# Attention in three-product precision: low parts on another engine, some squares on ScalarE, scores three blocks ahead, and the next batch prepared over two chunks

## The chip, the cores and the metric

The kernel runs on one core of a Trainium2 chip. A core has TensorE (PE, with its weight loads, PEld), VectorE (DVE), ScalarE (ACT), GpSimd (POOL) and SyncE (SP), each with its own queue that it works off in order, and DMA engines. Engines wait for each other by semaphores. The metric is the device time of one execution in microseconds; the kernel before takes 1697.85 us, the median of three runs (1695.41 to 1698.38).

## The reference

There is an attention without softmax, then two mixture-of-experts layers on its output:

```python
scores = scale * np.matmul(z, z.transpose(0, 2, 1))    # z: 4 x 3072 x 64, scale = 1/3072
attn = np.maximum(scores, 0.0) ** 2
x = u * np.matmul(attn, v)                              # u, v: 4 x 3072 x 256
logits = x @ moe_w_gate                                 # then a routing of 12288 tokens by capacity,
h = np.maximum(x[mask] @ w1[e], 0.0); y = h @ w2[e]     # 8 experts, and a second such layer
```

All tensors are fp32. The change touches the attention alone.

## The kernel before

**Precision.** A fp32 factor is split into a high part in TensorE's rounded fp32 format (fp32r) and a low part, the difference. A product is then three matmuls: high by high, low by high, high by low. So each of z, v, the squared scores and x has a copy on ScalarE (the high part: zHL's upper half, pH, aH, xH) and a subtraction (the low part: zHL's lower half, pL, aL, xL).

**Tiling.** The attention runs over 24 chunks: four batches of six chunks of 512 queries each. A chunk goes over 24 blocks of 128 keys (KT). For a block, `scores` makes two matmuls into a PSUM tile sc (zHL holds high part over low part, zLH the same two swapped), then r = relu(scale * sc) on ScalarE (L371), the full square a on VectorE (L377), the rounded square aH on ScalarE (L379) and aL = a - aH on VectorE (L381). `av` makes six matmuls into two accumulators (L396 aH by the high part of v, L397 aL by the high part, L398 aH by the low part, for two halves of d). After the 24th block VectorE multiplies each accumulator by u into xT (L400).

**What sets the order.** The program is recorded step by step, with no scheduler. Step s emits `scores(s + 2)`, then `av(s)`, then whatever a table of hooks holds for step s; each engine keeps that order. At the last block of a chunk the scores stand between the two halves (L401). Buffers: two of sc, r and a, four of aH and aL.

**Hooks of a chunk.** `turn_u` (a 32x32-block transpose of u on VectorE), `load_u`, `swap_z` (two DMAs from GpSimd's queue that make zLH of the next chunk), and of the chunk that has just ended `part_x` (xH on ScalarE, xL on GpSimd, L331), `logits` (four matmuls), `turn_l`, `put_l`, `put_x` (for the first ten chunks with two transposes rowb on VectorE). In the last chunk of a batch come the six z tiles and six v tiles of the next batch: `load_z`, `part_z` (VectorE transpose zT), `turn_z` (copy on ScalarE, low part on GpSimd, L281), `load_v`, `part_v` (copy pH on ScalarE L234, low part pL on GpSimd L235). The first batch's tiles are prepared in the first chunk in the same way, v in four pieces a tile. zHL and pH/pL have eight buffers, six for a batch and two to spare.

**The last batch** (chunks 18 to 23) also carries the first steps of the routing. There, blocks with an odd number have their full square on ScalarE (L375), so that VectorE has only aL. In the last chunk VectorE also splits four weight tiles of 128x1024 (at L235, with the copy on ScalarE).

Of the kernel before, what the change touches and what calls it, by code (L numbers as in the profile page):

```python
# [8 lines left out]
F32 = mybir.dt.float32  # L9
FR = mybir.dt.float32r  # L10
BF = mybir.dt.bfloat16
I32 = mybir.dt.int32
AF = mybir.ActivationFunctionType
OP = mybir.AluOpType
# [64 lines left out]
class Moe:  # L79
# [174 lines left out]
    def _attention(self, W, u, v, z, gates, stages, hooks):  # L254
        nc, S, B = self.nc, self.S, self.B
        KT, QC = S // 128, S // 512
        NC = B * QC
        zr, zT, zHL, vr, V, zLH, uraw, uT, xT, row, xp, lg = ({} for _ in range(12))

        def at(s, f, *a):  # L260
            hooks.setdefault(s, []).append((f, a))
# [13 lines left out]
        def turn_z(b, i):  # L275

            t = zHL[b, i] = W.tile([128, 512], FR, name="zHL", bufs=QC + 2)
            first = b == i == 0
            eng = nc.vector if first else nc.gpsimd
            nc.scalar.activation(t, zT[b, i], AF.Copy)  # L280
            eng.tensor_tensor(t[64:128], zT[b, i][64:128], t[64:128].bitcast(F32), OP.subtract)  # L281
            if first:
                l = zLH[0] = W.tile([128, 512], FR, name="zLH", bufs=2)
                nc.scalar.activation(l, zT[b, i], AF.Copy)
                eng.tensor_tensor(l[0:64], zT[b, i][0:64], l[0:64].bitcast(F32), OP.subtract)  # L285

        def swap_z(c):
            b, q = divmod(c, QC)
# [6 lines left out]
        VS = [128, 4, 256]  # L295
# [2 lines left out]
            vr[b, i] = self.load(v[b].rearrange("(i t p) d -> i p t d", p=128, t=4)[i], VS)  # L298

        def part_v(b, i):  # L300
            V[b, i] = self.split(vr[b, i], VS, nc.gpsimd, self.w, b == 0)

        def load_u(c):
            b, q = divmod(c, QC)
# [21 lines left out]
        def part_x(c, h):  # L326
            H = self.w.tile([128, 512], FR, name="xH", bufs=1)
            nc.scalar.activation(H, xT[c][:, h], AF.Copy)  # L328
            L = self.w.tile([128, 512], FR, name="xL", tag="xL", bufs=1)
            eng = nc.gpsimd if c < NC - 1 else nc.vector  # L330
            eng.tensor_tensor(L, xT[c][:, h], H.bitcast(F32), OP.subtract)  # L331
            xp[c, h] = H, L

        def logits(c, h):
# [25 lines left out]
        SCALE = 1.0 / S  # L360
        HS, LS = {}, {}

        def scores(s):
            c, k = divmod(s, KT)
            b = c // QC
            p = self.sc()
            lw = zHL[b, k // 4][:, k % 4 * 128:(k % 4 + 1) * 128]
            nc.tensor.matmul(p, lw, zHL[b, c % QC], start=True, stop=False)  # L368
            nc.tensor.matmul(p, lw, zLH[c], start=False, stop=True)  # L369
            r = W.tile([128, 512], F32, name="r", bufs=2)  # L370
            nc.scalar.activation(r, p, AF.Relu, scale=SCALE)  # L371
            a = W.tile([128, 512], F32, name="a", bufs=2)
            if b == B - 1 and k % 2:

                nc.scalar.activation(a, r, AF.Square)  # L375
            else:
                nc.vector.tensor_tensor(a, r, r, OP.mult)  # L377
            HS[s] = W.tile([128, 512], FR, name="aH", bufs=4)
            nc.scalar.activation(HS[s], r, AF.Square)  # L379
            LS[s] = W.tile([128, 512], FR, name="aL", bufs=4)  # L380
            nc.vector.tensor_tensor(LS[s], a, HS[s].bitcast(F32), OP.subtract)  # L381

        accs = None
# [1 line left out]
        def av(s):  # L385
            nonlocal accs
            c, k = divmod(s, KT)
            b = c // QC
            if k == 0:
                accs = [self.acc(), self.acc()]  # L390
            vh, vl = V[b, k // 4]
            if k == KT - 1:
                xT[c] = self.w.tile([128, 2, 512], F32, name="xT", bufs=1)
            for h in range(2):
                sl = (slice(None), k % 4, slice(h * 128, (h + 1) * 128))
                nc.tensor.matmul(accs[h], vh[sl], HS[s], start=k == 0, stop=False)  # L396
                nc.tensor.matmul(accs[h], vh[sl], LS[s], start=False, stop=False)  # L397
                nc.tensor.matmul(accs[h], vl[sl], HS[s], start=False, stop=k == KT - 1)  # L398
                if k == KT - 1:
                    nc.vector.tensor_tensor(xT[c][:, h], accs[h], uT[c][:, h], OP.mult)  # L400
                    if h == 0 and s + 2 < NS:  # L401
                        scores(s + 2)

        def put_l(c):
            for q in range(4):
# [3 lines left out]
        NS = NC * KT  # L409
        load_z(0, 0)  # L410
        load_v(0, 0)
        self.warm(12, self.mi())
        part_z(0, 0)
        turn_z(0, 0)
        load_z(0, 1)
        load_v(0, 1)
        load_u(0)
        part_v(0, 0)
        part_z(0, 1)
        tables = self.consts(*gates)  # L420
# [3 lines left out]
        for i in range(1, QC):  # L424
            d = 2 * (i > 2)
            at(4 * i - 4 - d, turn_z, 0, i)
            if i > 1:
                at(4 * i - 6 - d, part_z, 0, i)
                at(4 * i - 8 - d, load_z, 0, i)
                at(4 * i - 8, load_v, 0, i)  # L430
            at(4 * i - 3, part_v, 0, i)
        for c in range(NC):
            s0 = c * KT
            b, q = divmod(c, QC)
            if c + 1 < NC:
                at(s0 + 17, load_u, c + 1)
                at(s0 + 13, swap_z, c + 1)
            at(s0 + 12, turn_u, c, 0)
            at(s0 + 16, turn_u, c, 1)
            if c + 1 < NC:  # L440
                e = s0 + KT
                for t, f, a in ((0, part_x, (0,)), (2, logits, (0,)), (3, part_x, (1,)), (5, logits, (1,)),
                                (6, turn_l, ()), (8, put_l, ()), (9, put_x, ())):
                    at(e + t, f, c, *a)
            if q == QC - 1 and b + 1 < B:
                for i in range(QC):
                    at(s0 + 1 + 3 * i, load_z, b + 1, i)
                    at(s0 + 6 + 3 * i, part_z, b + 1, i)
                    at(s0 + 8 + 3 * i, turn_z, b + 1, i)
                    at(s0 + 4 * i - 6, load_v, b + 1, i)  # L450
                    at(s0 + 4 * i + 2, part_v, b + 1, i)
        for s in range(2):
            scores(s)
        for s in range(NS):
            if s + 2 < NS and s % KT != KT - 1:
                scores(s + 2)
            av(s)
            for f, a in hooks.pop(s, []):
                f(*a)
            for s0, p, c in stages:  # L460
                if p.done:
                    continue
                if s0 is None:

                    j = self.JP + 4 * (p.n // 5)
                    if s < (j // 4 + 1) * KT + 10:
                        break
                if s0 is None or s >= s0:
                    p.step(c)
                break  # L470
            if getattr(self, "pend", None):
                self.put_tail()
        for _, p, _ in stages:
            p.finish()
        c = NC - 1
        return [lambda: part_x(c, 0), lambda: (logits(c, 0), part_x(c, 1)), lambda: logits(c, 1),
                lambda: turn_l(c), lambda: put_x(c)]

# [1124 lines left out]
```

## Time and profile before

| | |
|---|---|
| median of three runs | 1697.85 us |
| profiled execution | 1710.32 us, its span 1708.5 us |
| TensorE busy | 1609.7 us, 94% of the span |
| VectorE busy | 1320.4 us, 77% |
| ScalarE busy | 1037.5 us, 61% |
| GpSimd busy | 508.8 us, 30% |
| mean granted TensorE clock | 0.982 of full speed |

How to read it: a share of busy time is a mean over stages. Matmuls are pipelined and a record of one (0.39 us) overlaps the next, so the pace of TensorE is read from the starts of neighbours (0.23 us), not from the lengths. The same holds for VectorE and ScalarE, whose records overlap by less than 0.1 us. The stretches below are cut where the second xT of a chunk ends; chunks are counted from 0, so that 5, 11 and 17 are those in which the next batch is prepared.

### The profile page before, as it was taken

How to read it: one execution, taken by the hardware profiler on the slowest of the kernel's cores; microseconds unless marked ns; L12 is line 12 of the kernel's file. 1: busy time of each engine (PE TensorE's matmuls, PEld its weight loads, DVE VectorE, ACT ScalarE, POOL GpSimd, SP SyncE). 2: the span in 40 equal slices, each digit the busy share in tenths (PEclk: the TensorE clock that was granted, in tenths of full speed). 3: DMA queues.
4: the chain of work that ended last, by engine and by line, in shares of the span. 5: the costliest groups of instructions: out<-in, count | busy, mean ns of one | idle time of the engine just before them, and what ended most of it. 6: DMA issues, size and time to landing. Idle time of an engine off the chain costs nothing.

```text
span 1708.5 us, 24999 instructions
## 1 busy us (share of the span) xinstructions
PE 1609.7 (94%) x8568; PEld 1323.5 (77%) x8570; DVE 1320.4 (77%) x2387; ACT 1037.5 (61%) x1777; POOL 508.8 (30%) x629
## 2 busy tenths in 40 slices
PE   8999998999999899999889999999999959999997
PEld 5788875788887588888667777767888849987997
DVE  8888889888888888888887777667777765776662
ACT  7666666666666566666677767766434315654552
POOL 6411014111112411011430278752333213324341
PEclk9999999999999999999999999999999969998999
DMA  5111255223224322212410111114334303553530
GB/s 124 29 29 31 41 144 132 56 76 78 70 56 107 85 56 57 56 45 48 105 40 13 33 33 37 26 41 134 107 107 126 99 15 101 185 163 101 162 122 31
DMA packets 282680, 132.43 MB, mean 78 GB/s; under 512 B 216717, under 2 KB 268173, under 8 KB 282544
## 3 DMA queue, kind: packets, MB, share of 16 engines
q1 hardware_dynamic: 269264, 106.90, 24.7%
q0 software_dynamic: 13280, 23.85, 4.8%
q8 instruction: 69, 1.13, 0.3%
q14 instruction: 67, 0.55, 0.1%
HBM read 84.61 MB, written 40.55 MB: 73 GB/s over the span
## 4 chain that ended last, share of the span: by engine, by line
PE 70%; DVE 19%; issue 4%; ACT 3%; POOL 1%; DMA 0%; another core or an unknown queue 0%; SPq 0%; DVEq 0%; POOLq 0%; ACTq 0%
PE acc L397 13%; PE acc L398 12%; PE acc L396 12%; PE sc L1010 9%; PE sc L368 6%; PE sc L369 6%; DVE aL L381 6%; PE acc L1160 5%; DVE a L377 5%; PE mi L1111 1%; ACT r L371 1%; DVE pL L225 1%; PE mi L338 1%; PE rt L863 1%; DVE hL L1020 1%
## 5 line engine op out<-in xcount | busy, mean ns | idle before, releaser
L371 ACT ACTIVATE r<-sc 128x512 f32<-128x512 f32 x576 | 343.6, 596 | 335.1 <-PE sc L369 300.5
L381 DVE TENSOR_TENSOR aL<-a,aH 128x512 fp32r<-128x512 f32 x576 | 447.4, 778 | 125.4 <-ACT aH L379 41.6
L397 PE MATMUL acc<-aL,pH 128*128 128x512 f32 x1152 | 460.5, 400 | 43.4 <-DVE aL L381 40.6
L377 DVE TENSOR_TENSOR a<-r 128x512 f32<-128x512 f32 x504 | 401.2, 796 | 70.2 <-ACT r L371 65.1
L396 PE MATMUL acc<-aH,pH 128*128 128x512 f32 x1152 | 451.6, 392 | 0.1
L398 PE MATMUL acc<-aH,pL 128*128 128x512 f32 x1152 | 451.4, 392 | 0.0
L379 ACT ACTIVATE aH<-r 128x512 fp32r<-128x512 f32 x576 | 363.3, 631 | 16.0
L397 PEld LDWEIGHTS acc<-aL,pH 128*128 128x128 f32 x1152 | 217.4, 189 | 120.5 <-DVE aL L381 75.6
L396 PEld LDWEIGHTS acc<-aH,pH 128*128 128x128 f32 x1152 | 217.5, 189 | 48.3 <-DVE xT L400 1.2
L398 PEld LDWEIGHTS acc<-aH,pL 128*128 128x128 f32 x1152 | 217.6, 189 | 42.9
L331 POOL TENSOR_TENSOR xL<-xT,xH 128x512 fp32r<-128x512 f32 x46 | 67.0, 1455 | 567.8 <-ACT xH L328 532.2
L368 PE MATMUL sc<-zHL 128*128 128x512 f32 x576 | 230.0, 399 | 5.4 <-ACT r L371 4.0
L369 PE MATMUL sc<-zLH,zHL 128*128 128x512 f32 x576 | 225.8, 392 | 0.2 <-DVE zLH L285 0.2
L1018 ACT ACTIVATE hH<-sc 128x432 fp32r<-128x432 f32 (+2 forms) x192 | 89.5, 469 | 216.6 <-PE sc L1010 201.4
L1020 DVE SCALAR_TENSOR_TENSOR hL<-sc,hH 128x432 fp32r<-128x432 f32 (+2 forms) x192 | 98.9, 523 | 67.6 <-ACT hH L1018 66.7
L368 PEld LDWEIGHTS sc<-zHL 128*128 128x128 f32 x576 | 109.1, 189 | 35.0 <-ACT r L371 4.8
L1010 PE MATMUL sc<-xTH,pH 128*128 128x384 f32 (+2 forms) x368 | 126.6, 344 | 7.0 <-DVE hL L1020 6.7
L369 PEld LDWEIGHTS sc<-zLH,zHL 128*128 128x128 f32 x576 | 109.0, 189 | 22.2 <-DVE zLH L285 0.5
L1010 PE MATMUL sc<-xTL,pH 128*128 128x384 f32 (+2 forms) x368 | 120.0, 326 | 0.0
L1010 PE MATMUL sc<-xTH,pL 128*128 128x384 f32 (+2 forms) x368 | 119.8, 326 | 0.0
L633 POOL DMA_INDIRECT tt<-TP,hidx x92 | 100.9, 1097 | 53.5 <-DVE ntail L653 25.8
L225 DVE TENSOR_TENSOR pL<-raw,pH 128x1024 fp32r<-128x1024 f32 x80 | 97.6, 1220 | 10.3 <-ACT pH L220 9.6
(335 smaller groups left out, 2153.0 us busy)
## 6 DMA issues: line engine op xcount, KB each, us to landing
raw<-in_moe_w_dram SPq DMA_DIRECT2D x84, 512.0 KB
raw<-in_v_dram SPq DMA_DIRECT2D x24, 512.0 KB
uraw<-in_u_dram SPq DMA_DIRECT2D x192, 64.0 KB
out_dram<-zt SPq DMA_DIRECT2D x24, 512.0 KB
xb<-xT SPq DMA_DIRECT2D x14, 512.0 KB
zr<-in_z_dram SPq DMA_DIRECT2D x96, 64.0 KB
zLH<-zHL POOLq DMA_DIRECT2D x46, 128.0 KB
ya<-zt SPq DMA_DIRECT2D x10, 544.0 KB
```

Of the source, the lines that this page charges most:

```text
L225: self.nc.vector.tensor_tensor(l, raw, h.bitcast(F32), OP.subtract)
L368: nc.tensor.matmul(p, lw, zHL[b, c % QC], start=True, stop=False)
L369: nc.tensor.matmul(p, lw, zLH[c], start=False, stop=True)
L371: nc.scalar.activation(r, p, AF.Relu, scale=SCALE)
L377: nc.vector.tensor_tensor(a, r, r, OP.mult)
L379: nc.scalar.activation(HS[s], r, AF.Square)
L381: nc.vector.tensor_tensor(LS[s], a, HS[s].bitcast(F32), OP.subtract)
L396: nc.tensor.matmul(accs[h], vh[sl], HS[s], start=k == 0, stop=False)
L397: nc.tensor.matmul(accs[h], vh[sl], LS[s], start=False, stop=False)
L398: nc.tensor.matmul(accs[h], vl[sl], HS[s], start=False, stop=k == KT - 1)
L1010: nc.tensor.matmul(p, a, b[:, d, :w], start=i == 0, stop=i == 5)
L1020: self.later.append(lambda: nc.vector.scalar_tensor_tensor(hL, p, 0.0, hH.bitcast(F32), op0=OP.max, op1=OP.subtract))
```

## The change

- The low parts of z, v and x are subtracted on VectorE instead of GpSimd, in all chunks.
- ScalarE makes the full square of every second block in the first chunk, in the last chunk of each batch and in the last batch (there as before), and of every third block elsewhere (k % 3 == 1). In these blocks aH now stands in front of a.
- `scores` runs three blocks ahead (LA) instead of two. aH and aL keep their four buffers.
- The hooks of the next batch are spread: the first z and v tile come 19 and 16 blocks before the last chunk of the batch begins, the second 6 and 3 before it, the other four within it, four blocks apart. `turn_z` comes one block after `part_z` instead of two. The distance from a load to its use stays five blocks for z and eight for v.

```diff
-            eng = nc.vector if first else nc.gpsimd
             nc.scalar.activation(t, zT[b, i], AF.Copy)
-            eng.tensor_tensor(t[64:128], zT[b, i][64:128], t[64:128].bitcast(F32), OP.subtract)
+            nc.vector.tensor_tensor(t[64:128], zT[b, i][64:128], t[64:128].bitcast(F32), OP.subtract)
...
         def part_v(b, i):
-            V[b, i] = self.split(vr[b, i], VS, nc.gpsimd, self.w, b == 0)
+            V[b, i] = self.split(vr[b, i], VS, nc.vector, self.w, b == 0)
...
-            eng = nc.gpsimd if c < NC - 1 else nc.vector
-            eng.tensor_tensor(L, xT[c][:, h], H.bitcast(F32), OP.subtract)
+            nc.vector.tensor_tensor(L, xT[c][:, h], H.bitcast(F32), OP.subtract)
...
+        LA = 3
...
-            if b == B - 1 and k % 2:
-
+            HS[s] = W.tile([128, 512], FR, name="aH", bufs=LA + 1)
+
+            if k % (2 if c == 0 or c % QC == QC - 1 or b == B - 1 else 3) == 1:
+                nc.scalar.activation(HS[s], r, AF.Square)
                 nc.scalar.activation(a, r, AF.Square)
             else:
                 nc.vector.tensor_tensor(a, r, r, OP.mult)
-            HS[s] = W.tile([128, 512], FR, name="aH", bufs=4)
-            nc.scalar.activation(HS[s], r, AF.Square)
-            LS[s] = W.tile([128, 512], FR, name="aL", bufs=4)
+                nc.scalar.activation(HS[s], r, AF.Square)
+            LS[s] = W.tile([128, 512], FR, name="aL", bufs=LA + 1)
             nc.vector.tensor_tensor(LS[s], a, HS[s].bitcast(F32), OP.subtract)
...
-                    if h == 0 and s + 2 < NS:
-                        scores(s + 2)
+                    if h == 0 and s + LA < NS:
+                        scores(s + LA)
...
                 for i in range(QC):
-                    at(s0 + 1 + 3 * i, load_z, b + 1, i)
-                    at(s0 + 6 + 3 * i, part_z, b + 1, i)
-                    at(s0 + 8 + 3 * i, turn_z, b + 1, i)
-                    at(s0 + 4 * i - 6, load_v, b + 1, i)
-                    at(s0 + 4 * i + 2, part_v, b + 1, i)
-        for s in range(2):
+                    t = s0 + (4 * i - 7 if i > 1 else 13 * i - KT + 5)
+                    at(t - 5, load_z, b + 1, i)
+                    at(t, part_z, b + 1, i)
+                    at(t + 1, turn_z, b + 1, i)
+                    at(t - 5, load_v, b + 1, i)
+                    at(t + 3, part_v, b + 1, i)
+        for s in range(LA):
             scores(s)
```

The order of VectorE at the end of chunk 4 and the first blocks of chunk 5 (a and aL are a block's square and its low part, zT, zHL, pL and xL belong to the preparation and to the chunk that ended). Before, from the first xT on:

```order
L400 TENSOR_TENSOR xT<-acc,uT 128x512
L377 TENSOR_TENSOR a<-r 128x512
L381 TENSOR_TENSOR aL<-a,aH 128x512
L400 TENSOR_TENSOR xT<-acc,uT 128x512
L377 TENSOR_TENSOR a<-r 128x512
L381 TENSOR_TENSOR aL<-a,aH 128x512
```

And now, from the same place:

```order
L401 TENSOR_TENSOR xT<-acc,uT 128x512
L379 TENSOR_TENSOR a<-r 128x512
L382 TENSOR_TENSOR aL<-a,aH 128x512
L401 TENSOR_TENSOR xT<-acc,uT 128x512
L382 TENSOR_TENSOR aL<-a,aH 128x512
L329 TENSOR_TENSOR xL<-xT,xH 128x512
L379 TENSOR_TENSOR a<-r 128x512
L382 TENSOR_TENSOR aL<-a,aH 128x512
L273 STREAM_TRANSPOSE zT<-zr 128x512
L382 TENSOR_TENSOR aL<-a,aH 128x512
L280 TENSOR_TENSOR zHL<-zT,zHL 64x512
```

Between the pairs of a and aL there now stand the low parts, and every second square is gone; before, that stretch goes on with six more pairs and nothing between them.

The order of ScalarE at the start of the program, from the first block's r to the copy of the second z tile. Before:

```order
L371 ACTIVATE r<-sc 128x512
L379 ACTIVATE aH<-r 128x512
L371 ACTIVATE r<-sc 128x512
L379 ACTIVATE aH<-r 128x512
L371 ACTIVATE r<-sc 128x512
L379 ACTIVATE aH<-r 128x512
L280 ACTIVATE zHL<-zT 128x512
```

And now:

```order
L371 ACTIVATE r<-sc 128x512
L380 ACTIVATE aH<-r 128x512
L371 ACTIVATE r<-sc 128x512
L376 ACTIVATE aH<-r 128x512
L377 ACTIVATE a<-r 128x512
L371 ACTIVATE r<-sc 128x512
L380 ACTIVATE aH<-r 128x512
L371 ACTIVATE r<-sc 128x512
L376 ACTIVATE aH<-r 128x512
L377 ACTIVATE a<-r 128x512
L279 ACTIVATE zHL<-zT 128x512
```

The copy stands behind four blocks and two full squares instead of behind three blocks.

## Rows read from the trace of the kernel before

**Rows 1.** Windows view: stretch; us, busy PE PEld DVE ACT POOL; PEclk, DMA, GB/s.

```profile
0.00:64.42 64.42, 56.93 (x219) 38.82 (x220) 55.14 (x69) 45.63 (x90) 40.78 (x52) 1.00 0.46 95
...
199.21:244.13 44.92, 44.80 (x197) 36.40 (x196) 38.24 (x56) 30.50 (x51) 4.71 (x5) 1.00 0.42 98
244.13:305.63 61.50, 49.52 (x200) 35.64 (x199) 58.20 (x62) 40.06 (x64) 30.93 (x18) 1.00 0.51 120
...
529.86:592.09 62.23, 50.77 (x196) 37.17 (x195) 57.37 (x61) 39.48 (x63) 30.88 (x18) 0.95 0.41 98
...
816.80:877.79 60.99, 50.38 (x199) 36.76 (x198) 56.35 (x59) 40.06 (x65) 30.94 (x18) 0.97 0.30 66
...
1132.07:1177.83 45.76, 44.83 (x198) 34.86 (x197) 35.13 (x60) 36.66 (x62) 26.71 (x39) 1.00 0.26 81
```

**Rows 2.** Waits view, 244.13 to 305.63 (engine line waited for: us, times, longest).

```profile
PE acc L397 <- DVE aL L381: 11.9, 11, 2.5
```

**Rows 3.** Lines view, 244.13 to 305.63 (columns: busy us, mean ns; idle us).

```profile
L377 DVE TENSOR_TENSOR a<-r 128x512 f32<-128x512 f32 x25 | 28.6, 1146 | 0.2 <-ACT r L371 0.2
L381 DVE TENSOR_TENSOR aL<-a,aH 128x512 fp32r<-128x512 f32 x24 | 24.7, 1028 | 3.1
...
L235 POOL TENSOR_TENSOR pL<-raw,pH 128x1024 fp32r<-128x1024 f32 x6 | 14.8, 2462 | 10.2 <-ACT pH L234 7.5 <-DVE a L377 2.6
```

**Rows 4.** Lines view, 484.93 to 529.86, an ordinary chunk.

```profile
L377 DVE TENSOR_TENSOR a<-r 128x512 f32<-128x512 f32 x25 | 17.8, 711 | 3.6 <-ACT r L371 3.4
L381 DVE TENSOR_TENSOR aL<-a,aH 128x512 fp32r<-128x512 f32 x24 | 17.6, 734 | 3.1
```

**Rows 5.** Timeline, 244 to 250 (start us, us, engine, line, operation).

```profile
248.46 2.41 POOL L235 TENSOR_TENSOR pL<-raw,pH 128x1024 fp32r<-128x1024 f32 x1 [2.57 <-DVE a L377]
248.56 2.85 DVE L381 TENSOR_TENSOR aL<-a,aH 128x512 fp32r<-128x512 f32 x1
```

**Rows 6.** Timeline of VectorE, undisturbed, near 255.

```profile
254.67 0.69 DVE L381 TENSOR_TENSOR aL<-a,aH 128x512 fp32r<-128x512 f32 x1
255.28 0.69 DVE L377 TENSOR_TENSOR a<-r 128x512 f32<-128x512 f32 x1
256.10 0.69 DVE L381 TENSOR_TENSOR aL<-a,aH 128x512 fp32r<-128x512 f32 x1
```

**Rows 7.** Timeline of ScalarE, 276 to 284.

```profile
277.94 1.04 ACT L234 ACTIVATE pH<-raw 128x1024 fp32r<-128x1024 f32 x1
278.89 0.58 ACT L371 ACTIVATE r<-sc 128x512 f32<-128x512 f32 x1
279.50 0.63 ACT L379 ACTIVATE aH<-r 128x512 fp32r<-128x512 f32 x1
280.04 0.58 ACT L371 ACTIVATE r<-sc 128x512 f32<-128x512 f32 x1
```

**Rows 8.** Timeline of VectorE, 1155 to 1180, a weight tile split.

```profile
1158.78 1.23 DVE L235 TENSOR_TENSOR pL<-raw,pH 128x1024 fp32r<-128x1024 f32 x1 [0.26 <-ACT pH L234]
1159.92 0.68 DVE L377 TENSOR_TENSOR a<-r 128x512 f32<-128x512 f32 x1
```

**Rows 9.** Timeline of TensorE behind the start of chunk 4.

```profile
201.05 0.39 PE L396 MATMUL acc<-aH,pH 128*128 128x512 f32 x1
...
201.56 0.50 PE L397 MATMUL acc<-aL,pH 128*128 128x512 f32 x1
...
201.90 0.40 PE L398 MATMUL acc<-aH,pL 128*128 128x512 f32 x1
```

**Rows 10.** Timeline of TensorE at the start of the program.

```profile
10.76 0.50 PE L397 MATMUL acc<-aL,pH 128*128 128x512 f32 x1 [0.70 <-DVE aL L381]
```

**Rows 11.** Waits view, 877.79 to 1177.83, the last six chunks.

```profile
PEld acc L397 <- DVE aL L381: 6.2, 10, 1.2
```

**Rows 12.** Timeline of VectorE at the start of the program.

```profile
6.17 0.69 DVE L281 TENSOR_TENSOR zHL<-zT,zHL 64x512 fp32r<-64x512 f32 x1 [0.70 <-ACT zHL L280]
6.89 0.69 DVE L285 TENSOR_TENSOR zLH<-zT,zLH 64x512 fp32r<-64x512 f32 x1
```

More of the change, by code (lines that the diff above doesn't have):

```diff
@@ L284, in turn_z @@
                 nc.scalar.activation(l, zT[b, i], AF.Copy)
-                eng.tensor_tensor(l[0:64], zT[b, i][0:64], l[0:64].bitcast(F32), OP.subtract)
+                nc.vector.tensor_tensor(l[0:64], zT[b, i][0:64], l[0:64].bitcast(F32), OP.subtract)
         def swap_z(c):
@@ L446, in _attention @@
                 for i in range(QC):
-                    at(s0 + 1 + 3 * i, load_z, b + 1, i)
-                    at(s0 + 6 + 3 * i, part_z, b + 1, i)
-                    at(s0 + 8 + 3 * i, turn_z, b + 1, i)
-                    at(s0 + 4 * i - 6, load_v, b + 1, i)
-                    at(s0 + 4 * i + 2, part_v, b + 1, i)
-        for s in range(2):
+                    t = s0 + (4 * i - 7 if i > 1 else 13 * i - KT + 5)
[5 more added lines that the diff above has]
+        for s in range(LA):
             scores(s)
         for s in range(NS):
-            if s + 2 < NS and s % KT != KT - 1:
-                scores(s + 2)
+            if s + LA < NS and s % KT != KT - 1:
+                scores(s + LA)
             av(s)
```

## The prediction

> **What bounds the kernel now.** I read the windows view first, cut where each chunk's second xT ends. A chunk that does nothing but attention (chunk 4 of the 24) takes 44.92 us, and TensorE is busy for 44.80 of it; the three chunks that also prepare the next batch take 61.50, 62.23 and 60.99; the first one ends at 64.42 [rows 1]. So in ordinary chunks TensorE is the bound, and nothing that the other engines save there counts, except where a wait stands. Together the three batch ends lose 184.72 - 3 x 44.92 = 50.0 us. The waits view of the first of them puts it on one place: L397, which needs aL, waits 11.9 us for VectorE's L381 [rows 2]. The lines view says why aL is late. There the square on VectorE (L377) takes 1146 ns on average and the low part (L381) 1028; in an ordinary chunk they take 711 and 734 [rows 3, 4]. That is 25 x 0.435 + 24 x 0.294 = 17.9 us of stretch, near the 16.6 us that this chunk loses. The timeline shows what stretches them: while GpSimd runs one low part of v for 2.41 us, the aL that starts 0.1 us after it takes 2.85 us, where an undisturbed one takes 0.69 [rows 5, 6]. GpSimd is busy for 30.93 us in this chunk, 14.8 of them with the six low parts of v, and for 4.71 in an ordinary one [rows 1, 3].
>
> **The change, part by part.**
>
> *Low parts of z, v, x to VectorE, preparation begun a chunk earlier, every second full square to ScalarE.* These act on the same 50.0 us, so I go by what each engine would have to do in such a chunk, in start-to-start times. VectorE: a block with both operations takes 0.82 + 0.61 = 1.43 [rows 6], a block whose square is ScalarE's 0.61. With twelve of each: 24.5. Two xT, two uT, one lgb, two rowb and two xL at 0.61 to 0.63: 5.6. Of the next batch four tiles are left in this chunk (two went to the one before): four zT 2.5, four low parts of z 2.4, four of v at 1.14 [rows 8] 4.6. Sum 39.6 of 44.92. ScalarE: r 0.61 and aH 0.54 per block, 27.6; twelve more squares at 0.54, 6.5; two xH 1.1, four copies of z 2.2, four of v at 0.95, 3.8 [rows 7]. Sum 41.2 of 44.92. Both fit as a whole. The tight part is the first 17 blocks (30.9 us of TensorE at 0.227 a matmul and eight a block, 31.8 with the logits and the chunk's start), since all of the preparation stands in them: VectorE 17 x 1.02 + 15 x 0.62 + 4.6 = 31.2, ScalarE 17 x 1.42 + 7.0 = 31.1. That is 98%, with the lead of three blocks on top of it. The nearest row that exists is the last chunk: there VectorE already has four tiles of this size to split, and ScalarE already makes every second square; it takes 45.76, 0.8 us over an ordinary one, with a lead of only two blocks [rows 1]. The new chunk has four z tiles and two xL more, so I leave 1.5 us of loss in each of the three: gain 50.0 - 4.5 = 45.5. Bounds: 50.0 if nothing is left, and 29 if the first 17 blocks' work queues so badly that 7 us stay in each.
>
> The moved instructions include DMA issues. SP gets to the z and v loads of the next batch up to a chunk earlier, in the same order of tiles and with the same distance to their use (five blocks for z, eight for v); buffers of z and v for the first two tiles are the two spare ones, so these loads wait for nobody. The chunk before takes two tiles: VectorE 16 x 1.43 + 8 x 0.61 + 5.6 + 4.8 = 38.1, ScalarE 27.6 + 8 x 0.54 + 1.1 + 3.0 = 36.0. It stays under TensorE's 44.92, and I cost it at nothing; if that cover failed, it would be a few us in each of three chunks.
>
> Against it, the Trainium skill ("VectorE: DVE Perf Modes", "Two Vector instructions with no wait between them") says that a VectorE instruction whose operand starts in another group of 32 partitions than the last one's starts only when all earlier ones have finished. The low part of z is on partitions 64 to 127. The trace agrees at the start of the kernel: behind it the next begins 0.72 us later, not 0.61 [rows 12]. By that, four such tiles would add about 8 x 0.11 = 0.9 us, and VectorE's 31.2 in the tight part would be 32.1. I leave the sum alone and give the first rival a little more.
>
> *Two xL of the ordinary chunks.* 23 chunks hand 46 of these to VectorE, at 0.61. Ordinary VectorE work is then 16 x 1.43 + 8 x 0.61 + 5.6 = 33.3 of 44.92, hidden beside TensorE. What goes is the stall at the chunk's start: GpSimd's xL stretches an aL there, and TensorE's next two starts are 0.51 and 0.34 after each other instead of 0.23 [rows 9], 0.39 us in each of the 14 ordinary chunks (1 to 4, 6 to 10, 12 to 16). Gain 5.5; bounds 0 and 5.5.
>
> *Scores three blocks ahead.* TensorE does the same matmuls. From the scores of a block to its use there are now 5.4 us and not 3.6, and the chain in between (r, square, low part) is about 3. So a stall below some 2 us disappears wherever VectorE and ScalarE catch up. In the last six chunks the weight load of L397 waits 6.2 us for aL [rows 11]; about 0.7 of such a wait reaches TensorE (0.39 of 0.55 in rows 9). Gain 4, bounds 0 and 6. Between the buffers nothing new is waited for: sc has two as before, and r two blocks back is read out long before.
>
> *The first chunk.* TensorE's first product with a low part starts at 10.76 [rows 10]; 24 blocks at 1.82 from there and the last xT would end it at about 55.3, and it ends at 64.42, so 9 us are lost. Two new waits appear. The second z tile is turned after the first block's products, and the scores that need it now come one block later instead of two. ScalarE has r, aH of blocks 0 to 3 and two full squares in front of it: 4 x 1.15 + 2 x 0.54 = 5.7 us from the first r at about 8.3; then the copy and VectorE's 0.69, about 15.3. TensorE is through with block 0 at about 12.2: 3.2 us. The third tile has r, aH and a of block 7 in front of it (0.61 + 0.54 + 0.54), the copy 0.63 and the subtraction 0.69, 3.1 after the scores, while one block's products are 1.4: 1.7 us. Behind each stand all of TensorE's products. The later tiles are turned two to three blocks earlier and don't bind. So about 4.9 of the 9 us stay: gain 4. VectorE's low part of a 128x256 piece has no row: from 0.31 (half of 128x512) to 0.61, 24 pieces 7.4 to 14.6; I take 0.35, nearest to what the step from 1.14 to 0.61 gives, and even 14.6 fits. Bounds for the chunk: -2 and 8.
>
> **Sum.** 45.5 + 5.5 + 4 + 4 = 59 us. The profiled execution took 1710.3, its span 1708.5, so that it should come to 1651; the median of the runs shown is 12.5 lower, at 1697.85, and the same 59 us off it give **1639 us**. All gains at their best are 69.5 (1628), all at their worst 27 (1671).
>
> **Rivals.**
> 1. *ScalarE and VectorE, both 98% full for 17 blocks, hold each other up.* For it: a block with both squares on ScalarE gives VectorE its input last, and r and a have two buffers each. Against it: the last chunk, and the lead. If they lose a quarter of their 31.2 us to each other (39.0 against 31.8), the lead takes some 2 of the 7.2 us and 5 stay at each batch end, 10.5 in all over what I left: 1649.
> 2. *The stretch isn't GpSimd's doing, so the change doesn't do what it says.* If VectorE's operations are long in these chunks for another reason (the loads, say), the 17.9 us come along, a third of them to the chunk before with its two tiles: 39.6 + 12 = 51.6, 6.7 over TensorE at each of three ends, and the ordinary stall stays: 30 + 4 gained, about 1664. Against it: in rows 5 the long operation ends 0.54 us after GpSimd's, about its own length.
> 3. *Slower: VectorE stands still for xH.* VectorE's queue runs in order. Each xL now stands there between a block's aL and the next square, and waits for ScalarE's xH, which stands behind r, aH and perhaps a. If VectorE is ahead, that is up to 0.61 + 0.54 + 0.54 + 0.54 = 2.2 us of standing still, 46 times, with every later square behind it: 101 us at the worst, 1740. It decides from 59 / 46 = 1.3 us that reach TensorE per xL. Against it: aL stands in the same place for aH, so most of that is no new wait, and VectorE has 11 us to spare in an ordinary chunk.
>
> **How the numbers follow.** Forecast 0.76, rival 1 0.14, rival 2 0.06, rival 3 0.03, 0.01 for what I don't see. The forecast alone ranges from 1628 to 1650. Two in ten may lie outside; I take in rival 1 and some way towards rival 2: 1627 to 1659. About 0.2% (3.4 us) is what a measurement of this kernel can tell from no change. The first three cases are all faster by far more: faster 0.95, the same 0.02, slower 0.03.
>
> **What would show it.** In the profile after: L381 and the VectorE square near 0.7 us in chunks 5, 11 and 17; these chunks at 45 to 47 us; ordinary ones at 44.5 without the wait behind the chunk's start; GpSimd almost idle until the last batch; in the first chunk two waits of L368 for zHL, and its end near 60. I am wrong if batch ends stay over 50 us, or if ordinary chunks grow past 45.

## The result and the profile after

The changed kernel takes 1637.64 us (median of four runs, 1634.53 to 1639.06) against 1697.88 us, a ratio of 0.9646 [0.9628, 0.9663]. The forecast was 1639 us, a gain of 59; measured are 60.2. The sum came out nearly right, and two of its four terms did not come from where I put them.

Two lines of the page show how the load moved: of the 40 slices of the span, GpSimd is busy for under a tenth of each from the second one until the last batch.

```profile
PE 1580.8 (97%) x8570; PEld 1326.7 (81%) x8570; DVE 1186.5 (73%) x2338; ACT 1116.7 (68%) x1937; POOL 333.1 (20%) x518
...
POOL 1000000000000000000000478642333113323341
```

VectorE took over GpSimd's subtractions and is still 133.9 us less busy than before (1320.4): its operations are no longer stretched, and 160 squares went to ScalarE (504 on VectorE before, 344 records of L379 now). The windows view of the changed kernel, cut as [rows 1]: the first chunk, an ordinary one, the three batch ends, the last chunk.

```profile
0.00:64.34 64.34, 56.79 (x222) 42.53 (x223) 47.41 (x87) 53.05 (x106) 7.88 (x23) 0.95 0.46 95
152.88:197.36 44.48, 44.48 (x197) 36.48 (x196) 32.50 (x51) 34.68 (x59) 1.51 (x3) 1.00 0.30 63
242.01:287.36 45.35, 45.11 (x197) 36.02 (x196) 39.27 (x58) 40.80 (x71) 1.97 (x3) 1.00 0.55 137
509.91:554.21 44.30, 44.30 (x197) 36.32 (x196) 38.08 (x56) 40.82 (x71) 1.96 (x3) 1.00 0.41 101
776.75:821.04 44.29, 44.29 (x197) 36.32 (x196) 38.08 (x55) 40.80 (x71) 1.96 (x3) 1.00 0.31 69
1063.27:1107.12 43.85, 43.85 (x197) 35.03 (x196) 32.51 (x61) 35.78 (x60) 21.80 (x32) 1.00 0.28 84
```

The three batch ends fell from 61.50, 62.23 and 60.99 us to 45.35, 44.30 and 44.29; in the last two TensorE is busy all through. The first chunk stayed as long as it was, and its granted clock is 0.95, where [rows 1] had 1.00. The lines view of the first batch end, beside [rows 3], shows both VectorE operations at their undisturbed length (columns: busy us, mean ns; idle us):

```profile
L382 DVE TENSOR_TENSOR aL<-a,aH 128x512 fp32r<-128x512 f32 x24 | 16.3, 687 | 5.1 <-ACT a L377 3.5
...
L379 DVE TENSOR_TENSOR a<-r 128x512 f32<-128x512 f32 x13 | 9.1, 698 | 0.1
```

And where [rows 2] had 11.9 us of waiting for aL, the waits view of TensorE and of its weight loads has one line each for the same chunk:

```profile
PE sc L368 <- ACT r L371: 0.2, 1, 0.2
```

```profile
PEld sc L368 <- ACT r L371: 1.5, 4, 0.7
```

**A second profile of before.** The profiled execution of before lies 12.5 us over the median, which the prediction carried along. So I profiled before once more.

> The kernel before, profiled a second time, unchanged. Its first profile has ScalarE standing for 6.2 us in chunk 22 without a releaser. If that belongs to that one execution, chunk 22 is 45 to 48 us here, the last six chunks 290 to 293 instead of 300.0, and the span near 1696. If it belongs to the kernel, they are 299 to 301 again.

That execution took 1697.52 us. Of its chunks only 21 and 22 differ by more than 1 us (49.39 and 45.72 for 52.57 and 52.68), and what follows the attention is 4.2 us shorter. First the windows row of chunk 22 in the profile of before, then in the second one, which has the last six chunks as well:

```profile
1079.39:1132.07 52.68, 48.20 (x199) 37.59 (x198) 30.36 (x54) 36.03 (x63) 31.22 (x53) 0.94 0.20 47
```

```profile
1077.79:1123.51 45.72, 45.20 (x201) 36.25 (x200) 30.32 (x54) 36.41 (x63) 32.24 (x53) 1.00 0.22 54
...
879.39:1169.28 289.89, 286.08 (x1385) 225.09 (x1384) 213.66 (x400) 218.68 (x371) 151.71 (x231) 1.00 0.18 42
```

In the first profile ScalarE stood still for 6.21 us in chunk 22, and the granted clock of that chunk is 0.94. The timeline of ScalarE there:

```profile
1111.79 0.61 ACT L379 ACTIVATE aH<-r 128x512 fp32r<-128x512 f32 x1
1118.61 0.60 ACT L371 ACTIVATE r<-sc 128x512 f32<-128x512 f32 x1 [6.21 <-remote]
```

The second profile has no such wait, so it was that execution's own, and below I compare with the second one. What lengthened chunk 21 stays open.

**Where the time went.** Lengths of chunks summed from the profiles, cut at the second xT of each (us; differences are taken before rounding):

| | before, second profile | after | difference | forecast |
|---|---|---|---|---|
| first chunk | 64.65 | 64.34 | -0.3 | -4 |
| batch ends (5, 11, 17) | 185.5 | 133.9 | -51.5 | -45.5 |
| 14 ordinary chunks | 629.3 | 622.8 | -6.5 | -5.5 |
| last six chunks | 289.9 | 286.1 | -3.8 | -4 |
| after the attention | 526.4 | 527.6 | +1.2 | 0 |
| sum | 1695.7 | 1634.8 | -60.9 | -59 |

### The profile page after: what moved, and what is told of

Same layout as the page of the kernel before. It is cut to its first block, busy times and chain, and to the rows that moved or that the text cites. A ratio compares the mean times of both kernels' runs of the same rounds, so it can differ in the third digit from the quotient of the medians.

```text
span 1634.8 us, 24914 instructions
## 1 busy us (share of the span) xinstructions
PE 1580.8 (97%) x8570; PEld 1326.7 (81%) x8570; DVE 1186.5 (73%) x2338; ACT 1116.7 (68%) x1937; POOL 333.1 (20%) x518
## 4 chain that ended last, share of the span: by engine, by line
PE 70%; issue 16%; DVE 7%; POOL 2%; ACT 2%; DMA 1%; SPq 1%; POOLq 0%; DVEq 0%
PE acc L397 12%; PE acc L398 12%; PE acc L399 12%; PE sc L1013 9%; PE sc L368 6%; PE sc L369 6%; PE acc L1163 5%; PE mi L1114 2%; DVE pL L225 1%; PE rt L866 1%; PE mi L336 1%; PE acc L1320 1%; PE acc L1321 1%; PE acc L1322 1%; DVE hL L1023 1%
## 5 line engine op out<-in xcount | busy, mean ns | idle before, releaser
L382 DVE TENSOR_TENSOR aL<-a,aH 128x512 fp32r<-128x512 f32 x576 | 398.6, 693 | 212.9 <-ACT a L377 157.8
L398 PE MATMUL acc<-aL,pH 128*128 128x512 f32 x1152 | 449.0, 390 | 0.0
L379 DVE TENSOR_TENSOR a<-r 128x512 f32<-128x512 f32 x344 | 238.5, 693 | 43.0 <-ACT r L371 41.8
L398 PEld LDWEIGHTS acc<-aL,pH 128*128 128x128 f32 x1152 | 216.7, 188 | 45.5
L347 POOL TENSOR_TENSOR lgs<-lgb 32x128 f32<-32x128 f32 x23 | 15.2, 659 | 853.2 <-DVE lgb L344 853.2
L377 ACT ACTIVATE a<-r 128x512 f32<-128x512 f32 x232 | 142.8, 616 | 0.0
```

## The experiments

All but two start from the changed kernel; the low parts alone and the second profile start from before. Ratios are to the kernel before, with 95% intervals; the chunk lengths are from each kernel's profile, in us.

| kernel | median us | ratio | first | ends | ordinary | last six |
|---|---|---|---|---|---|---|
| the change | 1637.64 | 0.9646 [0.9628, 0.9663] | 64.34 | 133.9 | 622.8 | 286.1 |
| low parts alone | 1664.12 | 0.9806 [0.9791, 0.9821] | 63.01 | 160.2 | 623.4 | 287.1 |
| low parts on GpSimd | 1658.57 | 0.9781 [0.9764, 0.9797] | 71.59 | 145.7 | 626.1 | 286.5 |
| old hooks | 1645.34 | 0.9694 [0.9675, 0.9713] | 65.87 | 142.4 | 621.3 | 285.4 |
| squares on VectorE | 1654.48 | 0.9758 [0.9741, 0.9774] | 67.62 | 146.9 | 623.2 | 286.2 |
| lead of two | 1633.04 | 0.9629 [0.9613, 0.9645] | 57.89 | 134.5 | 624.7 | 286.3 |
| GpSimd reads | 1639.36 | 0.9659 [0.9645, 0.9674] | 64.81 | 132.4 | 626.0 | 287.6 |
| GpSimd writes | 1637.34 | 0.9648 [0.9634, 0.9663] | 65.94 | 134.0 | 622.7 | 286.2 |
| z earlier | 1634.00 | 0.9627 [0.9614, 0.9640] | 61.02 | 133.9 | 622.8 | 286.2 |
| z earlier, fewer squares | 1633.23 | 0.9622 [0.9609, 0.9635] | 60.08 | 133.9 | 622.7 | 286.1 |
| lead two, then three | 1632.16 | 0.9620 [0.9607, 0.9633] | 60.01 | 133.9 | 622.6 | 286.2 |
| the same, z earlier, fewer squares | 1632.27 | 0.9618 [0.9605, 0.9631] | 60.89 | 134.0 | 622.8 | 286.2 |

The theory is that of the prediction: the batch ends were lost to GpSimd, whose low parts stretch VectorE's operations, and to VectorE's own work; the change takes the first away and spreads the second. The rivals were named there too.

**1. Low parts back on GpSimd.**

```diff
-            nc.vector.tensor_tensor(t[64:128], ...)
+            (nc.vector if first else nc.gpsimd).tensor_tensor(t[64:128], ...)
...
-            V[b, i] = self.split(vr[b, i], VS, nc.vector, self.w, b == 0)
+            V[b, i] = self.split(vr[b, i], VS, nc.gpsimd, self.w, b == 0)
...
-            nc.vector.tensor_tensor(L, xT[c][:, h], H.bitcast(F32), OP.subtract)
+            (nc.gpsimd if c < NC - 1 else nc.vector).tensor_tensor(L, ...)
```

> The changed kernel with the low parts of z, v and x subtracted on GpSimd again; lead, squares and spread hooks stay new. Theory (GpSimd's subtractions stretch VectorE's): in chunks 5, 11 and 17 VectorE's squares and low parts are back at 0.9 to 1.1 us a piece instead of 0.69, and the starts of ordinary chunks show a stretched aL again. GpSimd then has four v, four z and two x tiles in such a chunk, 4 x 2.46 + 4 x 1.59 + 2 x 1.5 = 19.2 us, of which 58% (17.9 of 30.9 before) would stretch: VectorE 24.5 + 4.4 + 2.5 + 11.1 = 42.5 of 44.9. So it nearly fits, and the time is only some us up: 1642 to 1654. Rival (the stretch has another cause, the transfers or the old order): VectorE's pieces stay near 0.69 to 0.75 and the time is 1630 to 1639.

Measured: 1658.57 us, slower than either theory said, on the side of the first. The stretch is back. The lines view of chunk 5 (250.39 to 299.72):

```profile
L379 DVE TENSOR_TENSOR a<-r 128x512 f32<-128x512 f32 x13 | 18.7, 1439 | 3.1 <-ACT r L371 2.9
...
L382 DVE TENSOR_TENSOR aL<-a,aH 128x512 fp32r<-128x512 f32 x24 | 18.2, 763 | 3.9 <-ACT a L377 2.2
...
L235 POOL TENSOR_TENSOR pL<-raw,pH 128x1024 fp32r<-128x1024 f32 x4 | 9.6, 2410 | 6.9 <-ACT pH L234 6.9
```

Against 698 and 687 ns that is 13 x 0.741 + 24 x 0.076 = 11.5 us of stretch, but the chunk is only 4.0 us longer (49.33 against 45.35). Ten of VectorE's operations, four low parts of z, four of v and two xL, are GpSimd's again, so the windows view has it busy for 42.27 us there, 3.0 more than in the change:

```profile
250.39:299.72 49.33, 45.57 (x194) 35.32 (x193) 42.27 (x48) 39.91 (x69) 19.15 (x13) 1.00 0.49 124
```

Another 7.3 us are in the first chunk, where the waits view has a place that I had not counted:

```profile
PEld sc L368 <- POOL zHL L280: 11.8, 5, 4.4
```

TensorE stands there for the low parts of z, which GpSimd makes late.

**2. Low parts alone on VectorE**, nothing else changed: kernel before with the three lines of the diff that name the engine.

```diff
-            eng = nc.vector if first else nc.gpsimd
+            eng = nc.vector
...
-            V[b, i] = self.split(vr[b, i], VS, nc.gpsimd, self.w, b == 0)
+            V[b, i] = self.split(vr[b, i], VS, nc.vector, self.w, b == 0)
...
-            eng = nc.gpsimd if c < NC - 1 else nc.vector
+            eng = nc.vector
```

> The kernel before with one part of the change alone: the low parts of z, v and x on VectorE. Theory (two things bound a batch end: GpSimd's hold on VectorE, and then VectorE's own work): VectorE's pieces go to 0.69 us, but a batch end still has 34.3 + 5.6 + 6 x 2.4 = 54.3 us of work for it, so it lasts 54 to 57 us instead of 61.6; the wait at the start of ordinary chunks goes (0.45 each). Time 1664 to 1676. Rival (GpSimd's hold was all): batch ends at 46 to 49, time 1638 to 1648.

Measured: 1664.12 us, at the theory's edge, with ends of 54.45, 53.27 and 52.47 us for 54 to 57. The windows view, the first batch end:

```profile
240.86:295.31 54.45, 48.74 (x200) 35.98 (x199) 51.05 (x74) 39.88 (x64) 3.00 (x3) 1.00 0.58 136
```

No operation is stretched (aL 693 ns, the square 690), and still the chunk takes 54.45, since VectorE is busy for 51.05 of it. So the low parts alone give 25.3 us at the three ends, and the 5.9 of the ordinary chunks, whose stall was GpSimd's alone.

**3. The old hooks, and the squares on VectorE.** Two kernels that undo one part each.

```diff
-                    t = s0 + (4 * i - 7 if i > 1 else 13 * i - KT + 5)
-                    at(t - 5, load_z, b + 1, i)
...
+                    at(s0 + 1 + 3 * i, load_z, b + 1, i)
+                    at(s0 + 6 + 3 * i, part_z, b + 1, i)
...
```

> The changed kernel with the next batch prepared within the last chunk of a batch, at the steps of the kernel before. Theory: what counts is the sum of work per engine and chunk: VectorE 24.5 + 5.6 + 6 x 2.4 = 44.4 of 44.5, ScalarE 27.6 + 6.5 + 1.1 + 6 x 1.5 = 44.2; both are full, so 2 to 6 us are lost in each of three chunks: 1644 to 1656. Rival (the lead of three blocks covers it, the spreading was not needed): 1636 to 1640.

```diff
-            if k % (2 if c == 0 or c % QC == QC - 1 or b == B - 1 else 3) == 1:
+            if b == B - 1 and k % 2 == 1:
```

> The changed kernel with the full squares on VectorE except in the last batch, as before. Theory: VectorE in a batch end has 24 x 1.43 + 5.6 + 9.5 = 49.4 of 44.5, 5 us over in each of three; the chunk before it has 44.7, full; the first has 34.3 + 15.8 = 50 of about 50. So 1650 to 1664. Rival (VectorE has room without GpSimd's hold, ScalarE's squares add nothing): 1636 to 1641.

Measured: 1645.34 and 1654.48 us, both within what the theory gave. One row of the windows view of each, the first batch end; first with the old hooks, then with the squares on VectorE:

```profile
243.36:291.61 48.25, 46.36 (x200) 36.72 (x199) 43.12 (x62) 44.51 (x76) 3.01 (x3) 1.00 0.65 155
```

```profile
245.89:295.91 50.02, 46.49 (x197) 35.87 (x196) 46.62 (x70) 35.06 (x59) 1.96 (x3) 1.00 0.51 124
```

The engine that carries the most is each time near the length of the chunk: ScalarE with 44.51 of 48.25, VectorE with 46.62 of 50.02. Undone singly, the three parts cost 11.7 (low parts), 8.4 (hooks) and 13.0 us (squares) at the ends, together 33.2, where the whole gave 51.5: they aren't additive, since all three change what VectorE has to do in the same chunks. The new order of aH and a was not undone by itself.

**4. A lead of two**, with the four buffers of aH and aL kept.

```diff
-        LA = 3
+        LA = 2
```

> The changed kernel with scores two blocks ahead. Theory: the lead covers bursts, so batch ends lose 2 to 5 us each and the last six chunks 3 to 8 us, while the first chunk gains about 3 us, since the scores that wait for the second and third z tile come a block later: 1643 to 1656. Rival (without GpSimd's hold nothing is left to cover): 1632 to 1637.

Measured: 1633.04 us. The theory, that the lead of three is worth several us, fell; the rival held. The last six chunks in the windows view, with a lead of two:

```profile
817.08:1103.40 286.32, 284.69 (x1385) 225.36 (x1384) 210.31 (x412) 219.07 (x372) 135.99 (x219) 1.00 0.18 43
```

286.3 against 286.1 with three and 289.9 before. The ends and the ordinary chunks are 0.5 and 2.0 us longer, and the first chunk is 6.5 shorter.

**5. GpSimd reading, GpSimd writing.** Is it GpSimd's being busy that holds VectorE, or its reading SBUF? Two kernels give it work that nobody uses, in every block of the twelve chunks 1 to 4, 7 to 10 and 13 to 16: one subtraction of 128x256, or three memsets of 128x256 and no operand. GpSimd waits for nobody in this work and does it in one stretch of 25 to 28 us per chunk, not block by block; some of chunk 1's share runs in the first chunk already.

```diff
+            if 0 < c % QC < QC - 1 and b < B - 1:
+                for t in range(KT):
+                    at(s0 + t, pool_reads)
```

> The changed kernel, and in twelve ordinary chunks GpSimd makes one subtraction of 128x256 per block from a constant tile in SBUF into a scratch tile that nobody reads. Theory (a GpSimd operation that reads SBUF holds up VectorE's two-input operations): VectorE's squares or low parts in these chunks go from 0.69 to 0.8 us or more on average, the sum of the stretch per chunk is 24 x 0.3 to 24 x 0.7 = 7 to 17 us, so that VectorE (33.3 of 44.5) gets to 40 to 50; these chunks last 44.5 to 51, time 1638 to 1715. Rival (the stretch came with the data that GpSimd and VectorE shared, or from the transfers): 0.69 as before, time 1636 to 1639.

> As the run with GpSimd's subtractions, but with three memsets of 128x256 per block, which read nothing. The Trainium skill (SBUF — State Buffer, SBUF: two separate sides) says that VectorE's two-input operations collide with GpSimd operations that read SBUF. If only reading counts, VectorE stays at 0.69 us and the time at 1636 to 1639. If writing counts as well, the stretch is like that of the subtractions.

The lines view from 110 to 195, first of the kernel in which it reads:

```profile
L315 POOL TENSOR_TENSOR dummy<-zt 128x256 f32<-128x256 f32 x48 | 45.2, 942 | 3.5
L387 DVE TENSOR_TENSOR aL<-a,aH 128x512 fp32r<-128x512 f32 x47 | 36.0, 766 | 11.0 <-ACT a L382 6.9
...
L384 DVE TENSOR_TENSOR a<-r 128x512 f32<-128x512 f32 x30 | 27.9, 930 | 3.1 <-ACT r L376 3.0
```

and of the kernel in which it only writes:

```profile
L316 POOL MEMSET dummy<- 128x256 f32 x142 | 44.4, 313 | 7.9
...
L388 DVE TENSOR_TENSOR aL<-a,aH 128x512 fp32r<-128x512 f32 x46 | 31.9, 693 | 17.0 <-ACT a L383 12.8
...
L385 DVE TENSOR_TENSOR a<-r 128x512 f32<-128x512 f32 x31 | 21.3, 688 | 5.4 <-ACT r L377 5.4
```

GpSimd is busy for 45.2 and 44.4 us, nearly the same. Where it reads, the square takes 930 ns instead of 689 and aL 766 instead of 693; where it writes, neither moves. This is what the Trainium skill ("SBUF — State Buffer", "SBUF: two separate sides") says: the ports that VectorE and GpSimd share are a lock held for a whole instruction, and a VectorE operation with two SBUF inputs meets it only against a GpSimd operation that reads SBUF. The traces agree: 930 against 688 ns here, and in [rows 5] the aL that starts 0.1 us after GpSimd's low part ends 0.54 us after it.

In time, 30 x 0.241 + 46 x 0.073 = 10.6 us of stretch from 110 to 195 vanish in VectorE's idle time, since chunks 2 and 3, in which that lies, keep their 44.47. The 3.3 us that the ordinary chunks lose with the reading are all in chunks 4, 10 and 16, which also carry two tiles of the next batch, and the ends behind them are 1.5 us shorter. The medians of both kernels can't be told from the change's. The windows view of the kernel that reads, chunks 3 and 4:

```profile
153.35:197.83 44.48, 44.48 (x197) 36.48 (x196) 37.38 (x51) 34.66 (x59) 24.03 (x27) 1.00 0.30 63
197.83:243.76 45.93, 45.73 (x200) 36.81 (x199) 41.55 (x56) 37.75 (x65) 19.09 (x21) 1.00 0.45 99
```

In the change VectorE is busy for 32.50 us of chunk 3 and 37.01 of chunk 4, and chunk 4 takes 44.65.

**6. The first chunk.** Four kernels try to get its 4 us back: the second and third z tile turned earlier; the same with every third block's square on ScalarE there instead of every second; a lead of two up to block 16 and three from there; and that with the other two.

```diff
+            if s == 0:
+                turn_z(0, 1)
...
-            if k % (2 if c == 0 or c % QC == QC - 1 or b == B - 1 else 3) == 1:
+            if k % (2 if c % QC == QC - 1 or b == B - 1 else 3) == 1:
```

> The changed kernel; in the first chunk the second z tile is turned right behind the first block's scores and the third at step 2 instead of 4, and the third z tile is loaded before u. Theory (the first chunk loses to the two waits of the scores for zHL and to the half clock that TensorE gets after them): no wait of L368 for zHL over 0.5 us, the clock full from 9 us on, first chunk 55 to 58 us instead of 64.3, time 1628 to 1632. Rival (ScalarE's queue, which has 46 us of work in this chunk, is the bound there, and the waits only show it): first chunk 61 to 64, time 1634 to 1638.

> As the run with the early z tiles, and ScalarE makes every third full square in the first chunk instead of every second. ScalarE has 2.2 us less, VectorE 3.3 us more (43.5 of about 46). If ScalarE is the tighter of the two there, 1 to 2 us faster than the run with the early z tiles (1627 to 1631); if VectorE is, 1 to 2 us slower; if TensorE is, the same.

```diff
-        for s in range(LA):
+        for s in range(2):
...
-            if s + LA < NS and s % KT != KT - 1:
+            if s < 16:
+                scores(s + 2)
+            elif s == 16:
+                scores(18)
+                scores(19)
+            elif s + LA < NS and s % KT != KT - 1:
```

> The changed kernel with scores two blocks ahead up to block 16 of the first chunk and three from there. Theory (the lead of three costs 6 us in the first chunk and gives 2 to 3 us elsewhere): first chunk as with lead 2 (58 us), all others as in the changed kernel (ordinary ones 622.7 us, batch ends 133.9), time 1629 to 1632, 2 to 4 us under the run with lead 2. Rival (the lead does nothing later, the difference was in the runs): 1633 to 1635, as with lead 2.

> As the run with lead 2 that becomes 3, and in the first chunk the second z tile is turned behind the second block's scores, the third at step 3, its load before u's, and ScalarE makes every third full square instead of every second. With lead 2 there were 2.4 us of waits for zHL and aL left in the first chunk; if they are the tiles' position, 1 to 2 us faster than that run (first chunk 56 to 57), otherwise the same.

Measured: 1634.00, 1633.23, 1632.16 and 1632.27 us. Turning z earlier alone came out at the edge of the rival, with a first chunk of 61.02. The two waits for zHL at these places are gone, but the half clock that the theory puts behind them came all the same, and now the weight loads of the scores wait for ScalarE's r. The waits view of the first chunk of that kernel, and its windows view from 12 to 20 us:

```profile
PEld sc L368 <- ACT r L371: 4.1, 3, 1.9
```

```profile
12.00:20.00 8.00, 8.00 (x27) 6.45 (x28) 6.23 (x13) 7.28 (x16) 5.53 (x11) 0.74 0.98 193
```

Fewer squares on ScalarE bring 0.8 us in the median, too little to be told from nothing. The lead of two that becomes three has a first chunk of 60.01, not the forecast 58, and turning z earlier in it as well brings nothing (60.89).

All four, and the lead of two, lie from 0.9618 to 0.9629, within each other's intervals. That is 0.17 to 0.29% under the change's, with intervals that still touch its own: they are probably a little faster, which isn't shown, and which of them is best can't be told.

## Why the prediction held, and where it did not

**The batch ends: mechanism right, the term mis-sized.** Measured 51.5 for 45.5. I left 1.5 us of loss in each end; measured are 45.35, 44.30 and 44.29 against 44.47 in an ordinary chunk, 0.5 us in all for my 4.5. That is 4.0 of the 6.0 us that I missed; about 1.3 are the stall at a chunk's start, which these three had as well and which I counted in the ordinary chunks alone, and 0.7 are the second profile's longer ends. The engine sums for the whole chunk held (39.6 and 41.2 us forecast, 39.27 and 40.80 busy in the windows above), but the 98% for the first 17 blocks did not. The windows view of the changed kernel, about the first 17 blocks of chunk 11 and the rest:

```profile
509.91:540.00 30.09, 30.09 (x135) 24.54 (x134) 26.63 (x39) 27.70 (x49) 1.96 (x3) 1.00 0.43 114
540.00:554.21 14.21, 14.21 (x64) 11.78 (x63) 11.46 (x18) 13.11 (x23) 0.00 (x0) 1.00 0.35 74
```

VectorE is busy for 26.63 of 30.09 there, with 39 instructions where I had counted 44: the fourth low part of v and one uT fall behind the 17th block, and chunk 11 has no rowb. Both engines are near 90%. The hold that the Trainium skill ("VectorE: DVE Perf Modes", "Two Vector instructions with no wait between them") speaks of is there: in chunk 5 the operations behind the four low parts of z start 0.72 us after them, as in [rows 12]. It didn't reach TensorE, which is busy all through chunks 11 and 17.

One reading behind this term was too simple. I set 17.9 us of stretch in chunk 5 beside the 16.6 that it loses, as if the one were the other. Experiment 2 takes all the stretch away and gains 25.3 of the 50 us, because VectorE then does the low parts itself (six tiles of each kind and two xL: 6 x 0.60 + 6 x 1.14 + 2 x 0.61 = 11.7 us an end); and experiment 1 brings 11.5 us of stretch back, takes ten operations off VectorE, and loses 4.0. The better measure is what VectorE is busy for in the chunk, and it costs before the engine is full. Three pairs show it: from 32.50 to 37.38 us cost nothing (chunk 3, GpSimd reading), from 37.01 to 41.55 cost 1.3 (chunk 4, the same), from 39.27 to 42.27 cost 4.0 (chunk 5, experiment 1).

**Ordinary chunks: right.** 6.5 for 5.5, 0.47 us a chunk. Experiment 2 gives 5.9 with the low parts alone, and the wide starts of [rows 9] are gone: in chunk 3 of the changed kernel TensorE is busy for 44.48 of 44.48. The two tiles that I costed at nothing in the chunk before a batch end make it 44.65 instead of 44.47.

**Scores three blocks ahead: the step failed, its number came from elsewhere.** The forecast was 4 us in the last six chunks "wherever VectorE and ScalarE catch up"; 3.8 came, but with a lead of two there are 3.6, the low parts alone give 2.8, and GpSimd's low parts with a lead of three give 3.4. So either brings most of it: the weight loads of the last six chunks wait 5.6 us for aL in the second profile of before, 2.3 with the low parts alone, 1.9 with a lead of two and not at all with a lead of three. (What the new order of aH and a does in the last batch, no run shows by itself.) I added the lead's gain to one that the low parts already had. By the profiles the lead of three gives 2.0 us in the ordinary chunks, most of it in chunks 4 and 10 (44.65 for 45.45 and 45.42), 0.5 at the ends and 0.2 in the last six, and costs 6.5 in the first. That makes it a loss, and the ratios point the same way (0.9646 and 0.9629), but their intervals overlap.

**The first chunk: waits right, sum wrong.** Both new waits are there. The timeline of the changed kernel at the two places, TensorE:

```profile
16.01 0.79 PE L368 MATMUL sc<-zHL 128*128 128x512 f32 x1 [2.70 <-DVE zHL L280]
16.61 0.63 PE L369 MATMUL sc<-zLH,zHL 128*128 128x512 f32 x1
17.03 0.63 PE L397 MATMUL acc<-aH,pH 128*128 128x512 f32 x1
...
26.87 0.50 PE L368 MATMUL sc<-zHL 128*128 128x512 f32 x1 [1.96 <-DVE zHL L280]
```

2.70 and 1.96 us, for 3.2 and 1.7. But the chunk ended at 64.34, not near 60. The step that failed is "24 blocks at 1.82 from there": it left the start of the products where it was, and the pace behind it. With a lead of three the scores of the fourth block stand in front of the first product, and as sc has two buffers, they wait for ScalarE's r of the second block. The timeline of the changed kernel, that r, these scores and the first product:

```profile
9.79 0.58 ACT L371 ACTIVATE r<-sc 128x512 f32<-128x512 f32 x1
10.43 0.79 PE L368 MATMUL sc<-zHL 128*128 128x512 f32 x1
11.45 0.63 PE L397 MATMUL acc<-aH,pH 128*128 128x512 f32 x1
```

Before, and with a lead of two, the first product starts 1.8 to 1.9 us earlier:

```profile
9.56 0.50 PE L396 MATMUL acc<-aH,pH 128*128 128x512 f32 x1
```

```profile
9.62 0.49 PE L397 MATMUL acc<-aH,pH 128*128 128x512 f32 x1
```

The pace stands in the rows of the two waits: the matmuls behind the first one start 0.60 and 0.42 us after each other instead of 0.23. The windows view, first of the changed kernel, then of the one with a lead of two (PEclk is the third number from the end):

```profile
0.00:12.00 12.00, 9.11 (x22) 4.05 (x23) 6.03 (x12) 7.05 (x13) 2.35 (x12) 0.86 0.77 165
12.00:20.00 8.00, 5.30 (x18) 3.96 (x17) 4.95 (x9) 5.46 (x13) 3.52 (x10) 0.78 1.00 192
20.00:30.00 10.00, 8.04 (x36) 6.30 (x35) 7.03 (x13) 7.56 (x16) 2.01 (x3) 1.00 0.60 139
```

```profile
0.00:12.00 12.00, 8.84 (x23) 3.65 (x24) 6.41 (x13) 7.22 (x14) 2.35 (x12) 1.00 0.84 167
12.00:20.00 8.00, 8.00 (x35) 6.32 (x35) 6.93 (x13) 7.87 (x17) 5.02 (x11) 1.00 1.01 183
20.00:30.00 10.00, 9.86 (x44) 7.82 (x43) 8.96 (x17) 9.81 (x21) 0.00 (x0) 1.00 0.89 209
```

By 30 us the changed kernel has made 22 + 18 + 36 = 76 matmuls, the other 102. The 26 between them are 5.9 us at 0.227, nearly all of the 6.5 by which the chunk is longer. Two windows of the changed kernel are below the full clock, 0.86 and 0.78: for a part of each the grant is the lower level (1.2 GHz). In the second one the slow starts follow the 2.70 us in which TensorE stood still; in the first one they come ahead of both waits. With a lead of two all three windows show 1.00, as [rows 1] had for the whole chunk.

The starts of TensorE's matmuls in the timeline say what each part costs. I add up over the first chunk, from the first product on, what a start comes later than 0.227 us after the last one, and keep apart the starts with over 0.1 us of waiting in front of them. Before, the first product is at 9.56, then 6.9 us are waits and 2.1 other late starts, together near the 9 us of the prediction. Now it is at 11.45, with 5.0 and 2.1. With a lead of two it is at 9.62, with 1.9 and 0.5. So the waits came as forecast (5.0 for 4.9), and the 1.9 us that they gained went into the later start. Against the lead of two, 1.8 of the 6.5 us are the later start, 3.1 the waits and 1.6 the other late starts; most of those of the changed kernel lie where the clock was low.

The misses, 6.0 us too little at the ends and 3.7 too much in the first chunk, with 1.2 behind the attention that I had at nothing, largely cancelled. That the total came within 2 us is in part luck.

**The rivals.** None of the three came. ScalarE and VectorE don't hold each other up (ends of 45.35 and under), experiments 1 and 5 show that the stretch is GpSimd's, and VectorE's standing still for xH, the slower case, costs an ordinary chunk nothing (44.47).

## What to carry to other kernels

Don't count a stretched operation as a loss by its length: ask how busy its engine is in that stage with the stretch. Here some 5 us of it cost nothing in an ordinary chunk in which VectorE was busy for 37 of 44.5 us, and at 42 of 44.5 it cost 4.0. When several edits ease the same wait, give the gain to one of them and cost the others at what is left, and undo them one at a time to see whether a part is still needed. A lead between the stages is filled once, at the start of the program: cost that fill where nothing else is there to hide it (here the first product came 1.9 us later).

## What the runs showed of the hardware

- The clock at the start: every kernel with a lead of three from the start has a stretch at 1.2 GHz within its first 32 us; the four profiles with a lead of two throughout (before twice, low parts alone, lead of two) have none there. But the kernel with a lead of two up to block 16, which has the order of the lead of two as far as that block, had one as well:

```profile
0.00:12.00 12.00, 8.67 (x21) 3.83 (x22) 6.18 (x12) 7.03 (x13) 2.35 (x12) 0.83 0.80 162
12.00:20.00 8.00, 8.00 (x31) 6.42 (x30) 5.63 (x12) 6.52 (x15) 5.15 (x11) 0.82 0.95 186
```

  (the windows view, its first 20 us), and a first chunk of 60.01 instead of 57.89. So neither the lead nor the order alone decides it, and what does stays open.
- First chunks that are made of the same instructions (the change, old hooks) took 64.34 and 65.87 us in their profiles, a difference of 1.5 us, while their chunks 2 and 3 took 44.47 in both. A difference of 1 us in the first chunk is not read from one profile.
